# Attention steps of a fused attention and MLP kernel laid out from one table, with a pair's seven sums inverted together and transposes a turn later

## The chip, the cores and the metric

The kernel runs on one core of a Trainium2 chip. The metric is the device time of one execution in microseconds (us). A core has TensorE (PE; its weight loads are PEld), VectorE (DVE), ScalarE (ACT), GpSimd (POOL) and SyncE (SP), which issues most DMAs. Each engine works through its own instructions in the order in which the program holds them; between engines, semaphores keep the order.

## The reference

Causal attention over 2 batches of 12 heads, 448 positions and 64 values a head, followed by two MLPs on the 896 tokens of 768 values. All is float32.

```python
scores = scale * np.matmul(q, k.transpose(0, 1, 3, 2))      # scale = 1/8, masked above the diagonal
scores = scores - np.max(scores, axis=-1, keepdims=True)
attn = np.exp(scores)
attn = attn / (np.sum(attn, axis=-1, keepdims=True) + 1e-09)
x = np.matmul(attn, v)                                      # then laid out as 896 x 768
h = np.maximum(x @ w_in, 0.0);  x = h * h @ w_out           # first MLP, d_ff = 2048
h = x @ w_in2;  out = h * (1 / (1 + np.exp(-1.702 * h))) @ w_out2
```

## The kernel before

The attention works on 12 pairs of heads, `n = 12`. The rows of a pair's scores (448 queries by at most 448 keys) are cut into blocks of 128 queries, of which only the keys up to the diagonal are computed, and the blocks into three groups. Group 0 holds the third block (128 x 384) and the first (128 x 128) of each head, group 1 the second block (128 x 256) of each head, group 2 the last 64 queries of both heads at once (128 x 448). For pair 0 alone groups 3 and 4 hold the two blocks of group 0 apart. So a pair has seven tiles of scores; each has a column in the small tile `stat` for its maximum, its sum and the sum's reciprocal.

The stages of a pair, with the names of the code:

- `scores(p, g)`: TensorE multiplies q and k into PSUM banks named s (L231 for group 2, L238 for the others).
- `shifted(p, g)`: VectorE reads each tile out of PSUM, adds the mask, scales by -1/8, writes it to SBUF (`pnh`, for group 2 `pnl`) and keeps the row's minimum in `stat` (L266).
- `exponentials(p, g)`: ScalarE takes the exponential in place, with that minimum as the bias, and accumulates the row's sum in `stat` (L283).
- `normalise(p, gs)`: VectorE adds 1e-9 to the sums of the groups gs (L293) and inverts them (L294); GpSimd then multiplies each tile by its reciprocals (L296).
- `transpose(p, g)`, g = 0 and 1: TensorE transposes 32 pieces of the pair's probabilities into four PSUM banks named t (L311).
- `keep_transposed(p, g)`: two banks are copied to the tile `pt`, one by ScalarE and one by VectorE (L316).
- `values(p)`: TensorE multiplies `pt` with v into the bank x (L335). `keep_values` casts it on ScalarE (L347), and `keep_rest` keeps what the cast lost on VectorE (L351).

The program is written out pair by pair, and what is written is the order on each engine. Turn p of the loop holds scores, reductions and exponentials of pair p + 2, the rest of the normalisation of pair p + 1, the transposes and copies of pair p, and the product x of pair p - 1. Ahead of the loop stand all of pair 0 and pair 1 up to the exponentials.

PSUM has eight banks, handed out in the order in which they are asked for, so that an instruction that opens a bank waits until the reader of the bank's last owner is done. `pnh` and `pnl` have three buffers each: a reduction of pair p + 2 writes where the probabilities of pair p - 1 lay.

Two other kinds of work stand in the loop. `some(k)` issues k steps of the weight decode: int64 words of the MLP weights are turned into two float32 parts by VectorE (L106, L108, L100, L102) and ScalarE (L105, L101). Turns 3 to 8 hold two chunks' worth of steps, turns 10 and 11 two more. `filler(p)` issues, in turns 10 and 11 only, which have no scores left, products of the first MLP's first block (`first_term`: L125, L126, L127, three matmuls each). After the loop `first_product` and `second_product` of both MLPs follow, which are matmuls of these three lines with casts, activations and decode beside them.

Of the kernel before, what the change touches and what calls it, by code (L numbers as in the profile page):

```python
# [14 lines left out]
ALU = mybir.AluOpType  # L15
# [3 lines left out]
B, H, S, D = 2, 12, 448, 64  # L19
# [16 lines left out]
WARM = 7  # L36


@with_exitstack
def attention_mlps_kernel(  # L40
# [11 lines left out]
    nc = tc.nc  # L52
# [63 lines left out]
    X = {}  # L116
# [21 lines left out]
    with tc.tile_pool(name="const", bufs=1) as cp, tc.tile_pool(  # L138
# [119 lines left out]
        def shifted(p, g):  # L258
# [4 lines left out]
            work.sort(key=lambda u: u[0])  # L263
# [23 lines left out]
        def normalise(p, gs, eng=nc.gpsimd):  # L287
            if p >= n:
                return
            st = stat[p]  # L290
            work = [u for g in gs for k in range(1 if g == 2 else 2) for u in units(p, g, k)]
            lo, hi = min(u[3] for u in work), max(u[3] for u in work) + 1
            nc.vector.tensor_scalar(st[:, 2, lo:hi], st[:, 1, lo:hi], 1e-9, None, op0=ALU.add)  # L293
            nc.vector.reciprocal(st[:, 2, lo:hi], st[:, 2, lo:hi])  # L294
            for _, _, pn, s, _ in work:
                eng.tensor_scalar(pn, pn, st[:, 2, s : s + 1], 1.0, op0=ALU.mult, op1=ALU.mult)  # L296

        def transpose(p, g):

            if g == 0:  # L300
                PT[p] = qk_p.tile([128, 2, 1024], F32, tag="pt", name="pt")
# [12 lines left out]
        def keep_transposed(p, g):  # L314
            for k, tp in enumerate(tbank.pop((p, g))):
                (nc.vector.tensor_copy if k else nc.scalar.copy)(PT[p][:, k, 512 * g : 512 * g + 512], tp)  # L316
# [38 lines left out]
        for g in (3, 1, 4, 2):  # L355
            scores(0, g)
            shifted(0, g)
            exponentials(0, g)
            if g == 4:
                normalise(0, (3, 1))  # L360
        normalise(0, (4,))
        scores(1, 0)
        scores(1, 1)
        shifted(1, 0)
        normalise(0, (2,), nc.vector)
        exponentials(1, 0)
        scores(1, 2)
        shifted(1, 1)
        exponentials(1, 1)
        shifted(1, 2)  # L370
        exponentials(1, 2)
        normalise(1, (0,))
# [5 lines left out]
        def filler(p):  # L378
            if p + 2 >= n:
                first_term(0, *spare_terms.pop(0), X)  # L380

        def some(k):
            for _ in range(k):
                if decode:
                    decode.pop(0)()

        for p in range(n):
# [19 lines left out]
            some(many)  # L407
            filler(p)
            shifted(p + 2, 1)
            exponentials(p + 2, 1)  # L410
            keep_transposed(p, 1)
            normalise(p + 2, (0,))
            some(many - 1)
            if p > 0:
                values(p - 1)
                keep_values(p - 1)
            filler(p)
            scores(p + 2, 2)
            shifted(p + 2, 2)
            exponentials(p + 2, 2)  # L420
            if p > 0:
                keep_rest(p - 1)
            some(many)
            filler(p)
            some(many - 1)
        first_term(0, 5, 0, X)
        values(n - 1)
        while decode:
            decode.pop(0)()
        keep_values(n - 1)  # L430
        keep_rest(n - 1)
# [144 lines left out]
```

## Time and profile before

| | us |
|---|---|
| runs | 551.65, 551.95, 560.81 |
| median of the runs | 551.95 |
| profiled execution, its own time | 551.52 |
| its span | 549.7 |
| busy in the span: PE | 538.6 |
| DVE | 354.0 |
| ACT | 268.0 |
| POOL | 69.3 |

The profile is of one execution. Its span runs from the first to the last instruction; what lies around it is 1.8 us. A matmul's end is modelled, so matmuls that follow each other overlap in their rows, and a busy TensorE is not a TensorE at its peak: how long a step keeps TensorE is read from the start of one group to the start of the next. The attention takes the first sixth of the span, the MLPs the rest, in which TensorE has no gaps.

### The profile page before, as it was taken

To read this page: it belongs to the slowest core of one execution; us is meant where nothing else is said; L and a number is where in the kernel's file an instruction comes from. 1 tells how busy PE (TensorE), PEld (TensorE's weight loads), DVE (VectorE), ACT (ScalarE), POOL (GpSimd) and SP (SyncE) were. 2 spreads that over 40 slices of the span, in tenths; PEclk is the share of its full clock that TensorE was granted. 3 is DMA by queue.
4 is the path that set the end of the run, shared out by engine and by line. 5 is a ranking of instruction groups with operands and counts; after the bars stand their busy time and mean duration, and the time that the engine had idled before them with its cause. 6 is when DMAs were issued, how large, how long until landed. Compare 5 with 4: busy or idle time off the path is not lost.

```text
span 549.7 us, 8778 instructions
## 1 busy us (share of the span) xinstructions
PE 538.6 (98%) x3199; PEld 479.4 (87%) x3199; DVE 354.0 (64%) x806; ACT 268.0 (49%) x610; POOL 69.3 (13%) x115
## 2 busy tenths in 40 slices
PE   8998899999999999999999999999999999999997
PEld 4665678999999999999999999999999999999996
DVE  6988976666666667555465467888878874544420
ACT  6988855666666564233222264555555432222210
POOL 5765630000000000000000011222221100000000
PEclk9999999999999999999999999999999999999999
DMA  7862113343334434333332234334334363443000
GB/s 219 284 188 89 32 30 95 107 116 97 105 115 125 139 129 154 122 109 110 120 86 85 59 87 116 100 103 115 113 109 143 120 199 107 140 148 116 33 35 33
DMA packets 25018, 62.30 MB, mean 113 GB/s; under 512 B 4496, under 2 KB 9744, under 8 KB 24976
## 3 DMA queue, kind: packets, MB, share of 16 engines
q1 hardware_dynamic: 24256, 61.17, 36.6%
q10 hardware_dynamic: 720, 0.57, 0.3%
q8 instruction: 25, 0.41, 0.3%
q14 instruction: 17, 0.14, 0.1%
HBM read 58.98 MB, written 2.75 MB: 112 GB/s over the span
## 4 chain that ended last, share of the span: by engine, by line
PE 89%; ACT 6%; DVE 3%; issue 1%; DVEq 0%; ACTq 0%
PE h L125 14%; PE y L127 14%; PE y L126 14%; PE h L127 14%; PE h L126 14%; PE y L125 14%; ACT pnh L283 4%; DVE pnh L266 2%; PE x L335 1%; ACT pt L316 1%; PE s L238 1%; ACT x L347 1%; PE warm L220 1%; PE s L231 1%; PE t L311 0%
## 5 line engine op out<-in xcount | busy, mean ns | idle before, releaser
L101 ACT CAST wsplit<-m 128x384 fp32r<-128x384 f32 (+1 forms) x112 | 62.7, 560 | 241.5 <-PE y L127 128.4
L125 PE MATMUL h<-x,wsplit 128*128 128x448 f32 x384 | 141.1, 367 | 0.0
L125 PE MATMUL y<-h,wsplit 128*128 128x448 f32 x384 | 140.2, 365 | 0.0
L127 PE MATMUL y<-h,wsplit 128*128 128x448 f32 x384 | 140.2, 365 | 0.0
L126 PE MATMUL y<-h,wsplit 128*128 128x448 f32 x384 | 140.2, 365 | 0.0
L126 PE MATMUL h<-x,wsplit 128*128 128x448 f32 x384 | 140.2, 365 | 0.0
L127 PE MATMUL h<-x,wsplit 128*128 128x448 f32 x384 | 140.2, 365 | 0.0
L102 DVE TENSOR_TENSOR wsplit<-m,wsplit 128x384 fp32r<-128x384 f32 (+1 forms) x112 | 68.8, 614 | 64.1 <-ACT wsplit L101 64.0
L100 DVE CUSTOM_DVE_ANT_0 m<-m,e 128x768 uint16<-128x768 uint16 (+1 forms) x112 | 78.9, 704 | 47.4 <-ACT e L105 34.1
L125 PEld LDWEIGHTS h<-x,wsplit 128*128 128x128 f32 x384 | 72.1, 188 | 6.1 <-DVE stat L293 0.2
L126 PEld LDWEIGHTS h<-x,wsplit 128*128 128x128 f32 x384 | 72.1, 188 | 5.8 <-issue 0.2
L125 PEld LDWEIGHTS y<-h,wsplit 128*128 128x128 f32 x384 | 72.1, 188 | 5.7
L127 PEld LDWEIGHTS y<-h,wsplit 128*128 128x128 f32 x384 | 72.1, 188 | 5.7
L127 PEld LDWEIGHTS h<-x,wsplit 128*128 128x128 f32 x384 | 72.1, 188 | 5.7
L126 PEld LDWEIGHTS y<-h,wsplit 128*128 128x128 f32 x384 | 72.1, 188 | 5.7
L108 DVE SCALAR_TENSOR_TENSOR m<-wraw,m 128x384 uint32<-128x384 uint32 (+1 forms) x112 | 70.3, 628 | 0.0
L105 ACT ACTIVATE e<-wraw 128x384 uint32<-128x384 uint32 (+1 forms) x112 | 67.8, 605 | 0.0
L473 POOL TENSOR_TENSOR h<-g,h 128x448 fp32r<-128x448 f32 x16 | 24.0, 1499 | 336.8 <-ACT h L468 336.8
L106 DVE TENSOR_SCALAR m<-wraw 128x384 uint32<-128x384 uint32 (+1 forms) x112 | 42.6, 380 | 0.0
L283 ACT ACTIVATE pnh<-pnh,stat 128x128 f32<-128x128 f32 (+2 forms) x72 | 35.7, 497 | 7.4 <-DVE stat L266 7.2
L296 POOL TENSOR_SCALAR pnh<-pnh,stat 128x384 f32<-128x384 f32 (+2 forms) x72 | 34.6, 500 | 28.0 <-ACT pnh L283 18.7
L468 ACT CAST h<-g 128x448 fp32r<-128x448 f32 x64 | 34.1, 568 | 3.7 <-DVE g L466 3.5
(54 smaller groups left out, 372.4 us busy)
## 6 DMA issues: line engine op xcount, KB each, us to landing
wraw<-w1i SPq DMA_DIRECT2D x32, 384.0 KB, 3.1
wraw<-w1o SPq DMA_DIRECT2D x24, 512.0 KB, 3.7
wraw<-w2i SPq DMA_DIRECT2D x32, 384.0 KB, 3.1
wraw<-w2o SPq DMA_DIRECT2D x24, 512.0 KB, 3.8
kr<-kT SPq DMA_DIRECT2D x11, 224.0 KB, 3.9
yT<-o SPq DMA_DIRECT2D x11, 224.0 KB, 2.0
v<-v SPq DMA_DIRECT2D x6, 384.0 KB, 3.9
qr<-qT SPq DMA_DIRECT2D x10, 224.0 KB, 4.1
```

The costliest lines, as they stand in the source:

```text
L100: tt(out=m, in0=m, in1=e, op=ALU.add)
L101: nc.scalar.copy(s[:, 0, :], w)
L102: rests.append(lambda: tt(out=s[:, 1, :], in0=w, in1=s[:, 0, :].bitcast(F32), op=ALU.subtract))
L105: lambda: nc.scalar.mul(e, lo, 2.0**-29),
L106: lambda: ts(m, hi, 3, 0x3FFFFFFF, op0=ALU.logical_shift_left, op1=ALU.bitwise_and),
L108: lambda: stt(m, in0=hi, scalar=0xC0000000, in1=m, op0=ALU.bitwise_and, op1=ALU.bitwise_or),
L125: nc.tensor.matmul(ps, ws[:, 0, w], rhs[:, 0, b, :], start=first, stop=False)
L126: nc.tensor.matmul(ps, ws[:, 0, w], rhs[:, 1, b, :], start=False, stop=False)
L127: nc.tensor.matmul(ps, ws[:, 1, w], rhs[:, 0, b, :], start=False, stop=last)
L283: nc.scalar.activation(pn, pn, ACTF.Exp, bias=st[:, 0, s : s + 1], scale=-1.0, accum_out=st[:, 1, s : s + 1])
L296: eng.tensor_scalar(pn, pn, st[:, 2, s : s + 1], 1.0, op0=ALU.mult, op1=ALU.mult)
L468: nc.scalar.copy(h[:, 0, b, :], gs[b])
```

## The change

Instead of calls written out, two tables of steps hold the order, `PROLOGUE` for what stands ahead of the loop and `TURN` for one turn. A step is a name and a pair: in `PROLOGUE` the pair itself, in `TURN` its distance from the turn. The new function `do` issues a step once; `s`, `min`, `exp`, `add`, `rec`, `nrm`, `T`, `kT`, `x`, `xc` and `xr` are scores, reductions, exponentials, the addition of 1e-9, reciprocals, scalings, transposes, copies, the product and its two read-outs. A letter behind a name gives the engine: D is VectorE, A is ScalarE, M alternates between them by the pair's number; h orders the four reductions of group 0 by head.

What differs in a turn p:

- The exponentials of group 0 are those of pair p + 1, whose reductions stand in the turn before; so are the reduction and exponential of group 2 and the exponentials of group 1.
- The seven sums of a pair are added to once, on GpSimd, at the end of a turn (`add012`), and inverted once, on VectorE, in the next (`rec012`); the seven scalings then follow each other on GpSimd (`nrm012`). Pair 0 keeps its additions on VectorE and in three parts.
- Transposes and copies are of pair p - 1, the product and its read-outs of pair p - 2, each a turn later. Two turns without scores follow the loop, 12 and 13; turns 10 and 11 keep their first terms.
- Of a pair's four copies one alternates, so that VectorE has two for an even pair and three for an odd one.
- Pair 0 starts with group 1.

```diff
+PROLOGUE = (
+    ("s1", 0), ("s4", 0), ("s3", 0), ("min1", 0), ("min4", 0), ("exp1", 0), ("s1", 1), ("min3", 0), ("min1", 1),
...
+TURN = (
+    ("exp0", 1), ("some1", 0), ("fill", 0), ("min2", 1), ("rec012", 0), ("nrm012", 0), ("s0", 2), ("exp2", 1),
...
-        def shifted(p, g):
+        def shifted(p, g, by_head):
...
-            work.sort(key=lambda u: u[0])
+            if not by_head:
+                work.sort(key=lambda u: u[0])
...
-        def normalise(p, gs, eng=nc.gpsimd):
-            if p >= n:
-                return
-            st = stat[p]
+        def places(p, gs):
+
             work = [u for g in gs for k in range(1 if g == 2 else 2) for u in units(p, g, k)]
-            lo, hi = min(u[3] for u in work), max(u[3] for u in work) + 1
-            nc.vector.tensor_scalar(st[:, 2, lo:hi], st[:, 1, lo:hi], 1e-9, None, op0=ALU.add)
-            nc.vector.reciprocal(st[:, 2, lo:hi], st[:, 2, lo:hi])
-            for _, _, pn, s, _ in work:
-                eng.tensor_scalar(pn, pn, st[:, 2, s : s + 1], 1.0, op0=ALU.mult, op1=ALU.mult)
+            return work, slice(min(u[3] for u in work), max(u[3] for u in work) + 1)
+
+        def sums(p, gs, eng):
+            _, at = places(p, gs)
+            eng.tensor_scalar(stat[p][:, 2, at], stat[p][:, 1, at], 1e-9, None, op0=ALU.add)
+
+        def reciprocals(p, gs):
+            _, at = places(p, gs)
+            nc.vector.reciprocal(stat[p][:, 2, at], stat[p][:, 2, at])
+
+        def normalise(p, gs, eng):
+            for _, _, pn, s, _ in places(p, gs)[0]:
+                eng.tensor_scalar(pn, pn, stat[p][:, 2, s : s + 1], 1.0, op0=ALU.mult, op1=ALU.mult)
...
-        def keep_transposed(p, g):
-            for k, tp in enumerate(tbank.pop((p, g))):
-                (nc.vector.tensor_copy if k else nc.scalar.copy)(PT[p][:, k, 512 * g : 512 * g + 512], tp)
+        def keep_transposed(p, g, k, eng):
+            copy = nc.scalar.copy if eng == "A" or (eng == "M" and p % 2 == 0) else nc.vector.tensor_copy
+            copy(PT[p][:, k, 512 * g : 512 * g + 512], tbank[p, g][k])
...
-            many = 2 if p > 9 else 1
-            scores(p + 2, 0)
-            scores(p + 2, 1)
-            shifted(p + 2, 0)
-            normalise(p + 1, (1, 2))
-            exponentials(p + 2, 0)
-            filler(p)
-            transpose(p, 0)
-            transpose(p, 1)
-            keep_transposed(p, 0)
...
+            for step, lag in TURN:
+                if step == "fill":
+                    filler(p)
+                elif step.startswith("some"):
+                    some(int(step[4:]) * (1 if p < 10 else 3))
+                elif p:
+                    do(step, p + lag)
+                else:
+
+                    for q in range(lag + 1):
+                        if q or step.startswith(("T", "kT", "x")):
+                            do(step, q)
+        for p in (n, n + 1):
+            for step, lag in TURN:
+                if p + lag < n and not step.startswith(("some", "fill")):
+                    if p + lag == n - 1 and step == "x":
+                        while spare_terms:
+                            first_term(0, *spare_terms.pop(0), X)
+                        first_term(0, 5, 0, X)
+                    do(step, p + lag)
```

How the order moves shows in three places. VectorE, one turn before, from the reduction of group 2 to the next pair's (names with pnl are group 2, with pnh groups 0 and 1; stat holds the sums, stat_336 and stat_441 those of two pairs; the numbers behind names are the tiles'):

```order
L266 ISA pnl0_128,stat_336<-s_428,last_124 128x448
...
L351 TENSOR_TENSOR x_411<-x_412,x_411 128x448
L266 ISA pnh1_126,stat_441<-s_442,mask_123 128x384
...
L293 TENSOR_SCALAR stat_336<-stat_336 128x3
L294 RECIPROCAL stat_336<-stat_336 128x3
L316 COPY pt_465<-t_467 128x512
L266 ISA pnh1_126,stat_441<-s_448,mask_123 128x256
...
L316 COPY pt_465<-t_485 128x512
L293 TENSOR_SCALAR stat_441<-stat_441 128x4
L294 RECIPROCAL stat_441<-stat_441 128x4
L266 ISA pnl1_129,stat_441<-s_533,last_124 128x448
```

The same stretch now, in a turn with three copies, from one subtraction of x to the next:

```order
L374 TENSOR_TENSOR x_736<-x_737,x_736 128x448
L283 ISA pnl1_129,stat_685<-s_766,last_124 128x448
...
L315 RECIPROCAL stat_580<-stat_580 128x7
L339 COPY pt_802<-t_804 128x512
L283 ISA pnh2_127,stat_794<-s_795,mask_123 128x384
...
L339 COPY pt_802<-t_803 128x512
L339 COPY pt_802<-t_821 128x512
L122 TENSOR_SCALAR m_777<-wraw_354 128x384
L283 ISA pnh2_127,stat_794<-s_866,mask_123 128x256
...
L374 TENSOR_TENSOR x_845<-x_846,x_845 128x448
```

Between the subtraction of x (L351, now L374) and the first reduction of the next pair's group 0 there now stand a reduction of group 2, the one reciprocal, which is of another pair, and a copy; the two additions are gone. L122 is a step of the decode.

GpSimd, one pair's scalings now (before, the four of group 0 and the three others stood in two parts, and the addition was VectorE's):

```order
L311 TENSOR_SCALAR stat<-stat 128x7
L319 TENSOR_SCALAR pnh_125<-pnh_125,stat 128x384
L319 TENSOR_SCALAR pnh_125<-pnh_125,stat 128x128
...
L319 TENSOR_SCALAR pnh_125<-pnh_125,stat 128x256 x2
L319 TENSOR_SCALAR pnl_128<-pnl_128,stat 128x448
```

The addition for the next pair stands behind this pair's last scaling.

TensorE now, from the last score (L247) on, with t the transposes, x the attention's product and h the first MLP's first terms:

```order
L247 MATMUL s<-kr,ql_89 128x448
L141 MATMUL h_1185<-x,wsplit 128x448
...
L334 MATMUL t<-ident,pnh_125 128x64 x24
L334 MATMUL t<-ident,pnl_128 128x64 x8
L358 MATMUL x<-pt,v_95 64x384 x2
...
L334 MATMUL t<-ident,pnh_126 128x64 x24
L334 MATMUL t<-ident,pnl_129 128x64 x8
...
L334 MATMUL t<-ident,pnh_127 128x64 x24
L334 MATMUL t<-ident,pnl_130 128x64 x8
```

Three sets of transposes and four products, of which the first product stands here, now follow the last score, where two and three did.

## Rows read from the trace of the kernel before

**Rows 1.** Busy time by stretch (us; count of instructions), granted TensorE clock, DMA share, GB/s.

```profile
18.71:67.48 48.77, 44.30 (x593) 30.26 (x593) 43.50 (x176) 42.95 (x143) 28.62 (x57) 1.00 0.44 136
24.49:30.15 5.66, 5.43 (x74) 3.72 (x74) 5.00 (x22) 5.21 (x19) 3.39 (x7) 1.00 0.68 223
55.07:61.47 6.40, 5.44 (x75) 3.72 (x75) 6.13 (x24) 5.20 (x18) 3.99 (x7) 1.00 0.04 7
200.00:300.00 100.00, 100.00 (x495) 92.68 (x495) 57.81 (x102) 33.32 (x61) 0.00 (x0) 1.00 0.36 113
```

**Rows 2.** Timeline of TensorE: start us, duration us, line, idle before and what ended it.

```profile
4.28 2.04 PE L238 MATMUL s<-kr,qr 64*128 64x128 f32 x12
...
18.71 1.98 PE L335 MATMUL x<-pt,v 128*64 128x384 f32 x28 [0.45 <-DVE stat L266]
...
30.15 1.98 PE L335 MATMUL x<-pt,v 128*64 128x384 f32 x28 [0.23 <-DVE stat L266]
32.06 1.02 PE L231 MATMUL s<-kr,ql 128*128 128x448 f32 x2
33.01 1.57 PE L238 MATMUL s<-kr,qr 64*128 64x384 f32 x12
34.41 1.15 PE L311 MATMUL t<-ident,pnh 64*128 64x64 f32 x24
...
69.39 1.02 PE L231 MATMUL s<-kr,ql 128*128 128x448 f32 x2
...
84.61 0.47 PE L125 MATMUL h<-x,wsplit 128*128 128x448 f32 x1
```

**Rows 3.** Waits from 18.71 to 67.48: total us, times, longest.

```profile
ACT pnh L283 <- DVE stat L266: 5.8, 8, 1.2
PE x L335 <- DVE stat L266: 4.9, 9, 1.0
...
DVE x L351 <- ACT x L347: 2.5, 6, 0.5
```

**Rows 4.** Timeline of ScalarE and VectorE around the end of a turn.

```profile
46.35 0.53 ACT L347 CAST x<-x 128x448 fp32r<-128x448 f32 x1
...
46.91 0.62 DVE L351 TENSOR_TENSOR x<-x 128x448 fp32r<-128x448 f32 x1 [0.47 <-ACT x L347]
...
47.45 0.55 DVE L266 CUSTOM_DVE_ANT_0 pnh<-s,mask 128x384 f32<-128x384 f32 x1
...
48.04 0.61 ACT L283 ACTIVATE pnh<-pnh,stat 128x384 f32<-128x384 f32 x1 [0.50 <-DVE stat L266]
...
48.82 0.17 DVE L293 TENSOR_SCALAR stat<-stat 128x3 f32<-128x3 f32 x1
```

**Rows 5.** VectorE's groups, 18.71 to 67.48: count | busy us, mean ns | idle before.

```profile
L316 DVE COPY pt<-t 128x512 f32<-128x512 f32 x16 | 10.7, 672 | 0.0
L266 DVE CUSTOM_DVE_ANT_0 pnh<-s,mask 128x384 f32<-128x384 f32 x16 | 8.2, 550 | 0.0
L266 DVE CUSTOM_DVE_ANT_0 pnh<-s,mask 128x256 f32<-128x256 f32 x16 | 6.1, 414 | 0.0
L266 DVE CUSTOM_DVE_ANT_0 pnl<-s,last 128x448 f32<-128x448 f32 x8 | 5.0, 625 | 2.0 <-PE s L231 2.0
...
L266 DVE CUSTOM_DVE_ANT_0 pnh<-s,mask 128x128 f32<-128x128 f32 x17 | 4.3, 284 | 0.0
L108 DVE SCALAR_TENSOR_TENSOR m<-wraw,m 128x384 uint32<-128x384 uint32 x2 | 1.5, 738 | 0.0
L294 DVE RECIPROCAL stat<-stat 128x4 f32<-128x4 f32 x8 | 1.4, 178 | 0.3
...
L293 DVE TENSOR_SCALAR stat<-stat 128x4 f32<-128x4 f32 x8 | 1.4, 173 | 0.0
```

**Rows 6.** GpSimd's scalings (timeline), VectorE's reciprocal ahead of one, and GpSimd's small memset (groups).

```profile
43.35 1.23 POOL L296 TENSOR_SCALAR pnh<-pnh,stat 128x256 f32<-128x256 f32 x2 [2.24 <-ACT pnh L283]
...
49.37 0.94 POOL L296 TENSOR_SCALAR pnh<-pnh,stat 128x256 f32<-128x256 f32 x2 [1.51 <-ACT pnh L283]
50.27 0.65 POOL L296 TENSOR_SCALAR pnl<-pnl,stat 128x448 f32<-128x448 f32 x1
...
51.17 0.18 DVE L294 RECIPROCAL stat<-stat 128x4 f32<-128x4 f32 x1
...
51.54 1.84 POOL L296 TENSOR_SCALAR pnh<-pnh,stat 128x384 f32<-128x384 f32 x4 [0.63 <-ACT pnh L283]
...
L215 POOL MEMSET pnl<- 128x64 f32 x3 | 0.3, 152 | 0.0
```

**Rows 7.** Timeline of VectorE at the start.

```profile
5.22 0.29 DVE L266 CUSTOM_DVE_ANT_0 pnh<-s,mask 128x128 f32<-128x128 f32 x1 [3.54 <-PE s L238]
...
10.95 0.45 DVE L296 TENSOR_SCALAR pnl<-pnl,stat 128x448 f32<-128x448 f32 x1
```

More of the change, by code (lines that the diff above doesn't have):

```diff
@@ L36 @@
 WARM = 7
+PROLOGUE = (
[4 rows of a table added]
+)
+TURN = (
[4 rows of a table added]
+)
 @with_exitstack
@@ L285, in exponentials @@
                 )
-        def normalise(p, gs, eng=nc.gpsimd):
-            if p >= n:
-                return
-            st = stat[p]
+        def places(p, gs):
             work = [u for g in gs for k in range(1 if g == 2 else 2) for u in units(p, g, k)]
-            lo, hi = min(u[3] for u in work), max(u[3] for u in work) + 1
-            nc.vector.tensor_scalar(st[:, 2, lo:hi], st[:, 1, lo:hi], 1e-9, None, op0=ALU.add)
-            nc.vector.reciprocal(st[:, 2, lo:hi], st[:, 2, lo:hi])
-            for _, _, pn, s, _ in work:
-                eng.tensor_scalar(pn, pn, st[:, 2, s : s + 1], 1.0, op0=ALU.mult, op1=ALU.mult)
+            return work, slice(min(u[3] for u in work), max(u[3] for u in work) + 1)
[8 more added lines that the diff above has]
+                eng.tensor_scalar(pn, pn, stat[p][:, 2, s : s + 1], 1.0, op0=ALU.mult, op1=ALU.mult)
         def transpose(p, g):
-            if g == 0:
+            if p not in PT:
                 PT[p] = qk_p.tile([128, 2, 1024], F32, tag="pt", name="pt")
@@ L353, in keep_rest, with do @@
             )
[L355 to L372, printed above, removed]
+        done = set()
+        def do(step, p):
+            if not 0 <= p < n:
+                return
+            name = step.rstrip("ADMh")
+            kind, gs = name.rstrip("0123456789"), [int(g) for g in name if g.isdigit()]
+            if kind in ("add", "rec", "nrm"):
+                if any((kind, p, g) in done for g in gs):
+                    return
+                done.update((kind, p, g) for g in gs)
+            elif (name, p) in done:
+                return
+            done.add((name, p))
+            on_vector = step.endswith("D")
+            if kind == "s":
+                scores(p, gs[0])
+            elif kind == "min":
+                shifted(p, gs[0], step.endswith("h"))
+            elif kind == "exp":
+                exponentials(p, gs[0])
+            elif kind == "add":
+                sums(p, gs, nc.vector if on_vector else nc.gpsimd)
+            elif kind == "rec":
+                reciprocals(p, gs)
+            elif kind == "nrm":
+                normalise(p, gs, nc.vector if on_vector else nc.gpsimd)
+            elif kind == "T":
+                transpose(p, gs[0])
+            elif kind == "kT":
+                keep_transposed(p, *gs, step[-1])
+            else:
+                {"x": values, "xc": keep_values, "xr": keep_rest}[kind](p)
+        for step, p in PROLOGUE:
+            do(step, p)
         load_qk(3)
@@ L378, in filler @@
         def filler(p):
-            if p + 2 >= n:
+            if p + 2 >= n and spare_terms:
                 first_term(0, *spare_terms.pop(0), X)
@@ L396, in attention_mlps_kernel @@
                 decode += split_w_steps(len(wsplit)) + [lambda i=len(wsplit) + 3: load_w(i)]
-            many = 2 if p > 9 else 1
-            scores(p + 2, 0)
-            scores(p + 2, 1)
-            shifted(p + 2, 0)
-            normalise(p + 1, (1, 2))
-            exponentials(p + 2, 0)
-            filler(p)
-            transpose(p, 0)
-            transpose(p, 1)
-            keep_transposed(p, 0)
[L407 to L427, printed above, removed]
+            for step, lag in TURN:
[5 more added lines that the diff above has]
+                    do(step, p + lag)
+                else:
+                    for q in range(lag + 1):
[9 more added lines that the diff above has]
+                    do(step, p + lag)
         while decode:
             decode.pop(0)()
-        keep_values(n - 1)
-        keep_rest(n - 1)
     hp_ = ctx.enter_context(tc.tile_pool(name="hp_", bufs=KF))
```

6 rows, old and new, of tables (PROLOGUE, TURN) are left out of this document.

## The prediction

> **What bounds the kernel now.** I read first which engine is full in which stretch. From 200 to 300 us, inside the two MLPs, TensorE is busy for all 100 us at the full granted clock, 495 matmuls or 0.202 us each, and VectorE and ScalarE are far from full [rows 1]. The diff touches nothing there. From the end of the attention's last product, where the next matmul starts at 84.61 [rows 2], to the end of the span at 549.73 are 465.12 us, and I carry them over unchanged. What the change can win is idle time of TensorE before 84.61.
>
> I then looked at one turn of the pair loop, from one product x to the next. Eight turns take 48.77 us [rows 1], 6.10 each. In the stretch from 24.49 to 30.15 TensorE has 5.43 us of work, and I take this as the floor of a turn: the product 1.91 (30.15 to 32.06), the score of the last query block 0.95 (to 33.01), the other scores 1.40 (to 34.41) [rows 2], and the rest, 1.17, the transposes. So eight turns hold 48.77 - 8 x 5.43 = 5.3 us that TensorE could save.
>
> The waits say who holds it back: product x waits 4.9 us for VectorE (for a bank that the score reductions free), ScalarE's exponentials wait 5.8 us for VectorE, VectorE's x subtraction waits 2.5 us for ScalarE [rows 3]. In order of time it is one loop over two engines: the cast of x on ScalarE starts at 46.35, x's subtraction on VectorE waits for it until 46.91, the next pair's first reduction comes behind it at 47.45, and the exponential waits for that until 48.04, with ScalarE idle for 0.50 [rows 4]. ScalarE's busy 5.21 us a turn and VectorE's 5.00 [rows 1] are each under 5.43; it is the hand-over between them that makes 6.10.
>
> **The change part by part.** *The loop is cut.* Exponentials of group 0 now belong to the pair whose reductions ran a turn earlier, so they stand behind finished work, and the subtraction of x has a product two pairs old before it. Behind the subtraction on VectorE stand only the last reduction, the reciprocal and a copy.
>
> *VectorE's work.* A turn loses two additions (0.17 each) and one reciprocal (0.18) [rows 5]: 0.52. The copies go from two to three in every second turn: half of 0.67, +0.34 [rows 5]. Over the eight turns VectorE's 43.50 [rows 1] becomes about 42.0, or 5.25 a turn, under TensorE's floor. The weight decode makes turns uneven: the turn with two of its steps holds 6.13 of VectorE work against 5.00 without [rows 1]. A plain turn comes to 5.00 - 0.52 = 4.48 with two copies and 5.15 with three; a step of up to 0.74 [rows 5] on top makes 5.9, 0.5 over TensorE's 5.43. Three or four turns of the eight lie over it, and part of that is taken up by the slack of their neighbours.
>
> *ScalarE's work.* It loses half a copy a turn. It stands once a turn at the cast of x, whose product ends 0.93 + 1.17 + 1.91 = 4.0 us into TensorE's turn; the exponentials and the copy ahead of it are done by then, or some 0.1 late where a decode step is among them. This wait costs nothing while exp1, behind it, still reaches GpSimd before VectorE wants the reciprocal.
>
> *GpSimd.* Its seven scalings take 1.84 + 0.94 + 0.65 = 3.43, and its start comes 0.19 after the reciprocal's end (51.17 + 0.18 to 51.54) [rows 6]. The added addition on 128x7 is not in the trace; a 128x64 memset of 0.15 bounds it from below [rows 6], and half the pair of 128x256 scalings, 0.47 [rows 6], from above. I take 0.2, as it is nearest to the memset in size. The loop from reciprocal to reciprocal is then 0.18 + 0.19 + 3.43 + 0.2 + 0.19 = 4.2, or 4.5 with the upper price; both lie under 5.43, so it is covered. If ScalarE came late, VectorE would stand at the reciprocal with a copy, four reductions and a bank that TensorE needs behind it. The Trainium skill (GPSIMD Engine Reference, Engine selection) speaks against this move: elementwise work belongs on VectorE, GpSimd being about twice as slow with two inputs and about line rate with one. By that the addition would cost the row's 0.17 to 0.34, inside my bounds, and the sum would not change.
>
> *Transposes a turn later.* In the kernel before they wait for scalings that GpSimd gets late. Now the reciprocal stands about 1.2 us into a turn, so the scalings end near 4.8, and the transposes that need them come 5.43 + 0.93 = 6.4 us after its start. That gives 1.6 us of slack; the price if it goes is what is missing, on TensorE's path, in each turn.
>
> *The front.* VectorE's first reduction starts at 5.22 [rows 7], and I put it 0.4 later, since a 256-wide block now goes first. Its queue ahead of pair 1's reciprocal is three pairs of reductions, 23.6 us for eight pairs by the busy column or 2.95 each [rows 5], or 2.6 by group 0's four of 1.56, which ran in 1.37 start to start (47.45 to 48.82) [rows 4, 5]. To these come three additions, three reciprocals and one scaling of 0.45 [rows 7], 1.5 in all. That ends between 5.6 + 7.8 + 1.5 = 14.9 and 16.0; I take 14.9, as the reductions stand back to back as in that row. The reciprocal 0.18, a hand-over 0.19, scalings 3.43, the last eight of 32 transposes 0.3 and two more hand-overs 0.4 follow: x of pair 0 starts at 19.4 (19.0 to 20.3), against 18.71 before. But TensorE has by then also done a score of 0.95 and one of 0.93 (1.40 x 512/768) that came later before, so the front gains 18.71 + 1.88 - 19.4 = 1.2.
>
> *The tail.* After its last scores the kernel before needs 84.61 - (69.39 + 0.95) = 14.27 [rows 2] for two sets of transposes, three products and nine first terms. The changed order has one more set (1.17) and one more product (1.91) left: 17.35. They stand in front of the wait: the last pair's exponentials, reciprocal and scalings end about 10.7 us after the last score, and TensorE's work ahead of its transposes is 8 x 0.61 + 2 x 1.17 + 2 x 1.91 = 11.0. So I cost the longer drain at nothing, with only 0.3 us of cover; if it is gone, up to 3.4 us of scalings would show.
>
> *Sum.* A turn I put at 5.55: the floor of 5.43 and 0.12 for turns that VectorE fills over. There are now seven from the first product to that of the last turn with scores, then product and remaining scores 1.91 + 0.47 + 0.95. 19.4 + 7 x 5.55 + 3.33 + 17.35 + 465.12 = 544.05 of span. The profiled execution took 551.52 with a span of 549.73, so 1.8 lie around it, and its time is 0.4 under the median of the three runs, 551.95: **545.8 us**, about 1.1% less.
>
> **The rivals.**
> *The loop closes again (550 us).* VectorE and ScalarE are both within 0.3 us of the floor, and any hand-over that I have not seen eats it. For it: the decode turns that are 0.5 too full. Against: in the new order each wait has half a turn of slack. A turn of 6.10: 19.4 + 42.7 + 3.33 + 17.35 + 465.12 + 1.8 = 549.7, with the late front 550.6. Chance 19%.
>
> *GpSimd sets the turn (553.5 us, slower than before).* Place: the run of seven scalings, now between two reciprocals that VectorE waits for. The row for it: beside a decode step a pair of 128x256 scalings took 1.23 instead of 0.94 [rows 6], 0.29 more. GpSimd had idle time for this before; now the run is in a loop. Were all seven struck, it would be 3.43 + 7 x 0.29 = 5.46, and the loop 5.46 + 0.18 + 2 x 0.19 + 0.2 = 6.2, or 6.5 with the upper price. It decides from 5.43 on, so from four or five struck scalings a turn. With 6.3 a turn, 20.0 at the front and 1.8 that shows in the tail: 20.0 + 44.1 + 3.33 + 17.35 + 1.8 + 465.12 + 1.8 = 553.5. The Trainium skill (SBUF — State Buffer, two separate sides) gives the rule: VectorE, with two SBUF inputs or in a two-port mode, and GpSimd hold one port pair by turns, each for a whole instruction. The trace agrees in kind, 0.29 in a row. Reductions, copies and x read PSUM, so by it only decode steps strike. The rows say the same of how often: GpSimd's 28.62 in eight turns [rows 1] are 8 x 3.43 + 1.2, four strikes in all. Chance 8%.
>
> *TensorE without a gap (543 us).* Turns at 5.43, the front at 19.0 and a tail of 16.6, which is its pieces without switching: 19.0 + 38.0 + 3.33 + 16.6 + 465.12 + 1.8 = 543.9, and some 0.7 less if the front closes up too. Chance 9%.
>
> That the change does not do what its words say I leave out: the order shows one reciprocal over seven sums and transposes of the pair before.
>
> **How the numbers follow.** Forecast 62%, loop closes again 19%, no gap 9%, GpSimd 8%, something unseen 2%. The range takes in the forecast with its own bounds (543.5 to 547.5), most of the gapless case and the loop case to its late front: 543.0 to 550.6. Left out are about 5% below and 10% above. 2%, about what a measurement of this kernel can tell from no change, is 11.0 us. TensorE's own attention work is about 12 x 5.43 + 9 x 0.61 = 70.7, done between 4.28 and 84.61 [rows 2]: all its idle time is 9.6 us. So faster by over 2% has 3%; slower by over 2% (over 563) needs a turn of 7.4 us, 3%; within 2% the rest.
>
> **What would show it.** Right: products x 5.5 us apart from the second turn on; the waits of exponentials for VectorE and of x's subtraction for ScalarE gone or under 1 us in all; GpSimd in one run of seven a turn and its addition near 0.2; the first product near 19.4, the first MLP matmul behind the last product near 79. Wrong: VectorE standing at the reciprocal for GpSimd for more than 0.5 us a turn (then the first or second rival), transposes waiting for GpSimd, a gap of TensorE ahead of the last transposes, or the MLP part not 465 us long.

## The result: 547.0 us, and the profile after

Six runs of the changed kernel gave 546.32 to 547.61 us, median 546.96; six of the kernel before had the median 551.68. The ratio is 0.9916 (95% interval 0.9903 to 0.9929), a gain of 0.8%; the forecast was 545.8. The profiled execution took 547.05, with a span of 545.3. Some executions come out about 9 us longer, which two traces below show to lie in the matmuls of the MLPs (485 in 100 us for 496) and not in the attention, so ratios leave them out, and where they move a median the lowest run stands beside it.

Busy time by stretch in the changed kernel, against [rows 1]: seven turns, a turn with one step of the weight decode on VectorE, a turn with two, a piece of the MLPs. The columns are those of [rows 1].

```profile
20.57:59.49 38.92, 38.92 (x521) 25.76 (x519) 37.22 (x138) 35.11 (x120) 25.90 (x57) 1.00 0.52 157
26.13:31.69 5.56, 5.56 (x78) 3.68 (x75) 5.20 (x20) 5.06 (x17) 3.56 (x9) 1.00 0.91 278
42.81:48.37 5.56, 5.56 (x77) 3.68 (x75) 5.56 (x22) 5.56 (x21) 2.90 (x7) 1.00 0.15 49
200.00:300.00 100.00, 100.00 (x496) 92.68 (x495) 57.22 (x103) 30.95 (x56) 0.00 (x0) 1.00 0.37 113
```

TensorE is busy for all 38.92 us of the seven turns, where before it had 44.30 of 48.77. Each turn takes 5.56. Its timeline, against [rows 2]:

```profile
13.69 1.14 PE L254 MATMUL s<-kr,qr 64*128 64x384 f32 x8 [1.48 <-DVE stat L283]
...
18.50 1.14 PE L254 MATMUL s<-kr,qr 64*128 64x384 f32 x8 [1.23 <-DVE stat L283]
...
20.57 1.98 PE L358 MATMUL x<-pt,v 128*64 128x384 f32 x28
...
31.69 1.98 PE L358 MATMUL x<-pt,v 128*64 128x384 f32 x28
33.60 0.70 PE L254 MATMUL s<-kr,qr 64*128 64x256 f32 x4
34.23 1.02 PE L247 MATMUL s<-kr,ql 128*128 128x448 f32 x2
35.18 1.14 PE L254 MATMUL s<-kr,qr 64*128 64x384 f32 x8
36.15 0.92 PE L334 MATMUL t<-ident,pnh 64*128 64x64 f32 x24
...
37.25 1.98 PE L358 MATMUL x<-pt,v 128*64 128x384 f32 x28
...
62.03 1.02 PE L247 MATMUL s<-kr,ql 128*128 128x448 f32 x2
...
80.16 0.47 PE L141 MATMUL h<-x,wsplit 128*128 128x448 f32 x1
```

From start to start a turn is product 1.91, block 1's scores 0.63, the last group's 0.95, blocks 0's 0.97, transposes 1.10: 5.56 with no bracket, so no wait. The two score groups, 1.40 in one piece in [rows 2], cost 1.60 apart. The transposes last as long as before: 1.10 to the start of the next product, or 1.17 to their modelled end at 37.32, which is how the prediction's 1.17 was read. The two brackets left are in the front.

Waits from 20.57 to 62.98, against [rows 3]: those three are gone. GpSimd waits for the last exponentials and for the reciprocal, ScalarE for the products; in the whole list no engine waits for GpSimd, and no matmul for anything.

```profile
POOL stat L311 <- ACT pnh L300: 5.8, 7, 1.5
POOL pnh L319 <- DVE stat L315: 4.8, 5, 1.9
ACT x L370 <- PE x L358: 4.7, 6, 1.3
```

The sum of the prediction beside the trace: first product 20.57 for 19.4; seven turns 38.92 for 38.85; then to the end of the last scores (62.98) 3.49 for 3.33; tail 17.18 for 17.35; MLPs 465.1 for 465.12. The miss is the front's 1.17; the others cancel to within 0.1.

### The profile page after: what moved, and what is told of

Its sections match the earlier page's. It is cut to its first block, busy times and chain, and to the rows that moved or that the text cites. A ratio compares the mean times of both kernels' runs of the same rounds, so it can differ in the third digit from the quotient of the medians.

```text
span 545.3 us, 8723 instructions
## 1 busy us (share of the span) xinstructions
PE 538.0 (99%) x3199; PEld 478.0 (88%) x3199; DVE 352.6 (65%) x779; ACT 265.4 (49%) x604; POOL 73.1 (13%) x126
## 4 chain that ended last, share of the span: by engine, by line
PE 97%; DVE 2%; issue 0%; ACT 0%; ACTq 0%; DVEq 0%
PE h L141 14%; PE y L142 14%; PE h L143 14%; PE y L141 14%; PE h L142 14%; PE y L143 14%; PE x L358 4%; PE s L254 3%; PE t L334 2%; PE s L247 2%; DVE pnh L283 1%; PE warm L236 1%; DVE pnl L283 0%; DVE pt L339 0%; DVE stat L315 0%; DVE pnl L319 0%
## 5 line engine op out<-in xcount | busy, mean ns | idle before, releaser
L122 DVE TENSOR_SCALAR m<-wraw 128x384 uint32<-128x384 uint32 (+1 forms) x112 | 43.3, 387 | 0.0
L300 ACT ACTIVATE pnh<-pnh,stat 128x384 f32<-128x384 f32 (+2 forms) x72 | 35.6, 501 | 2.0 <-DVE stat L283 2.0
```

The lines of the kernel that those rows point to most:

```text
L122: lambda: ts(m, hi, 3, 0x3FFFFFFF, op0=ALU.logical_shift_left, op1=ALU.bitwise_and),
L300: nc.scalar.activation(pn, pn, ACTF.Exp, bias=st[:, 0, s : s + 1], scale=-1.0, accum_out=st[:, 1, s : s + 1])
```

## The experiments

Each is an edit of one of the two kernels. Two questions were open: which part took the turn from 6.10 to 5.56, and what held the front.

### The exponentials back in their own turn

```diff
-("exp0", 1), ("min2", 1), ... ("exp2", 1), ... ("exp1", 1), ... ("s2", 2)
+("min0h", 2), ("exp0", 2), ... ("min1", 2), ("exp1", 2), ... ("s2", 2), ("min2", 2), ("exp2", 2)
```

> The changed kernel with its exponentials back in the turn of their scores (each right behind the reduction of the same group, and the last group's reduction right behind its scores), everything else kept: sums on GpSimd in one go, transposes a turn later. Theory A (the prediction's): what held the turn of the kernel before at 6.10 us was the loop in which ScalarE's exponentials wait for VectorE's first reduction and VectorE's subtraction for ScalarE's copy of the products, and letting the exponentials lag by a turn is what cut it. Then ScalarE waits for VectorE again, some 5 us over the seven turns, and the turn is 5.75 to 6.1: 548.3 to 550.7. Rival B: the deeper pipeline of normalisation and transposes alone is what freed TensorE, the order of the exponentials is covered, the turn stays at 5.56 and the time at 547.0.

547.00 us, ratio 0.9913 (0.9898 to 0.9927). Seven turns took 38.92 again, and of the old waits this much came back (20.53 to 59.45):

```profile
DVE x L374 <- ACT x L370: 1.6, 3, 0.9
...
ACT pnh L300 <- DVE stat L283: 0.6, 1, 0.6
```

Rival B holds: the lag of the exponentials did not shorten the turn.

### The two score groups together

```diff
-("s0", 2), ("exp2", 1), ... ("exp1", 1), ("s1", 2),
+("s0", 2), ("s1", 2), ("exp2", 1), ... ("exp1", 1),
```

> The changed kernel with the scores of query block 1 put right behind those of blocks 0 (both groups of 64-row matmuls together, as in the kernel before), all else as it is. Theory A: the changed kernel's turn of 5.56 us is TensorE's own pace with no wait in it, and 0.20 of it comes from the two score groups standing apart (0.64 + 0.97 in the changed kernel against 1.40 together before). The turn falls to 5.36 to 5.43 us and the time by 7 x 0.13 to 0.20 us, to about 545.8. Rival B (the prediction's own reading): the 0.12 over 5.43 are turns that VectorE fills over, so the turn stays at 5.5 to 5.56 with TensorE now waiting for VectorE. Rival C: the earlier scores find their bank of PSUM not yet read, TensorE waits for VectorE's reductions, and the turn grows to 5.8 or more: 548.7 or more.

Ratio 0.9949 (0.9935 to 0.9964), about 548.8 us; the lowest run is 548.34. A turn of TensorE (of the next turn's products the last row holds the first two matmuls):

```profile
26.94 1.98 PE L358 MATMUL x<-pt,v 128*64 128x384 f32 x28 [0.28 <-DVE pt L339]
...
29.80 1.57 PE L254 MATMUL s<-kr,qr 64*128 64x384 f32 x12
31.21 0.91 PE L334 MATMUL t<-ident,pnh 64*128 64x64 f32 x24
...
32.65 0.54 PE L358 MATMUL x<-pt,v 128*64 128x384 f32 x2 [0.28 <-DVE pt L339]
```

The scores do take 1.41 in one piece, so Theory A's 0.20 is there, but the products stand 0.28 in five of the seven turns, and a turn is 5.71, 5.75 in the mean: TensorE waits for VectorE as in rivals B and C, at a size between theirs. What ends the wait is VectorE's copy of a transposed bank (26.20 to 26.89). The reductions that read the first scores run from 26.80 on and are not done when the products start at 26.94, so it was a bank of the transposes that was missing, not that of the first scores, as the expectation of the run with an earlier first reduction has it. All other parts of the change, without this one, bring about 2.8 of the 4.7 us.

### Block 1's scores behind the products, in the kernel before

```diff
             scores(p + 2, 0)
-            scores(p + 2, 1)
...
+            scores(p + 2, 1)      # and shifted, exponentials, normalise(p + 2, (0,))
             scores(p + 2, 2)
```

> The kernel before with one part of the change alone: the scores, reduction and exponentials of query block 1 come behind the products of the turn, not right behind the scores of block 0. Sums, reciprocals, scalings, the pair that a turn transposes and the place of the subtraction stay as before. Two runs have left this open: the exponentials back in their own turn cost nothing, and the two score groups together brought a TensorE wait of 0.29 us a turn at the first product back. Theory A: banks of PSUM are given out in turn, eight of them and ten requests a turn, so with both score groups ahead the products take the bank of the first scores of the same turn and must wait for their reduction on VectorE; with block 1 behind the products they take a bank that was read a turn ago. Then the wait of TensorE for VectorE ahead of the products (4.9 us over the turns) is gone, and the turn falls from 6.10 to 5.6 to 5.75 us: 548.2 to 549.2. Rival B (the prediction's loop): ScalarE's copy of the products, VectorE's subtraction, the first reduction and the first exponential still follow one another from turn to turn, and the turn stays at 6.0 to 6.1: 550.9 to 551.7.

547.04, ratio 0.9917 (0.9905 to 0.9929): the whole gain, from one part. Every turn from the first is 5.56, in the changed kernel's order and durations:

```profile
17.61 1.98 PE L335 MATMUL x<-pt,v 128*64 128x384 f32 x28
19.52 0.70 PE L238 MATMUL s<-kr,qr 64*128 64x256 f32 x4
20.16 1.02 PE L231 MATMUL s<-kr,ql 128*128 128x448 f32 x2
...
23.17 1.98 PE L335 MATMUL x<-pt,v 128*64 128x384 f32 x28
```

The edit moves three things: the order of TensorE's banks, the place of block 1's exponentials on ScalarE, and that of its reductions on VectorE, which come behind a copy. The next two runs take the first two one at a time.

### Banks alone: the first reductions head by head, in the kernel before

```diff
-            work.sort(key=lambda u: u[0])
+            if g or p < 2:
+                work.sort(key=lambda u: u[0])
```

> The kernel before with the four reductions of blocks 0 (and their exponentials) taken head by head from pair 2 on, so that the first head's bank, which the products take next, is read after two of the four (0.55 and 0.28 us) and not after three (two of 0.55 and one of 0.28); nothing else is moved. It shortens the way from the first reduction to the products by about 0.5 us and leaves the way through ScalarE as long as it was. Theory A, the loop that sets the turn of 6.10 us is closed by that bank (first reduction, products, copy on ScalarE, subtraction on VectorE, first reduction): the turn falls to about 5.65 and the time to about 548.4. Theory B, the loop is closed through ScalarE's own order (the first exponential waits for the first reduction, and the copy of the products stands behind that turn's exponentials): TensorE only waits less ahead of the products and more elsewhere, the turn stays at 6.0 to 6.1, 551 to 551.7.

Lowest run 551.25, ratio 0.9997 (0.9987 to 1.0008). Turns stay 6.10 (48.76 for eight). The subtraction on VectorE (L352; L348 is the cast, each a line later than before) and the transposes behind it:

```profile
46.83 0.62 DVE L352 TENSOR_TENSOR x<-x 128x448 fp32r<-128x448 f32 x1 [0.53 <-ACT x L348]
...
47.60 0.43 PE L312 MATMUL t<-ident,pnh 64*128 64x64 f32 x7 [0.44 <-DVE x L352]
```

The waits from 18.71 to 67.48:

```profile
DVE x L352 <- ACT x L348: 5.1, 8, 1.0
...
PE t L312 <- DVE x L352: 2.1, 6, 0.5
...
PE x L336 <- DVE stat L267: 1.5, 4, 0.6
```

Ahead of the products TensorE waits 1.5 us for VectorE instead of 4.9 [rows 3]. In its place stand 2.1 inside the transposes, for a bank that the subtraction still holds, and the subtraction waits 5.1 for ScalarE instead of 2.5. Theory B by the time. The chain that ended last, followed back from the last instruction through what released each step, does run over TensorE here in four of the eight turns, by the bank of the subtraction; so the run shows that the first scores' bank did not set the turn, not that no bank could.

### ScalarE's order alone: block 1's exponentials behind the copy of the products

```diff
-            exponentials(p + 2, 1)
             keep_transposed(p, 1)
...
                 keep_values(p - 1)
+            exponentials(p + 2, 1)
```

> The kernel before with one thing moved on ScalarE alone: the two exponentials of query block 1 come behind the copy of the products. The order of TensorE, of the banks and of VectorE stays. Theory A, the bank closes the loop: the products still wait for the first reduction, the turn stays at 6.0 to 6.1, 551 to 551.7. Theory B, ScalarE's order closes it: the copy of the products stood behind 0.99 us of those exponentials; it and the subtraction on VectorE come about 0.5 us earlier, since the subtraction stands behind the last group's reduction then; VectorE no longer waits for ScalarE there (2.5 us over the turns before), and the turn falls to 5.6 to 5.8: 548.2 to 549.6.

548.30, ratio 0.9942 (0.9930 to 0.9955): Theory B. From 18.96 to 58.80 seven turns take 5.69 each, 5.44 and 5.45 in the two without decode steps and 5.5 to 5.9 in the others. TensorE's products, the cast and the subtraction in a plain turn:

```profile
24.40 1.98 PE L335 MATMUL x<-pt,v 128*64 128x384 f32 x28
...
26.68 0.52 ACT L347 CAST x<-x 128x448 fp32r<-128x448 f32 x1
...
28.01 0.62 DVE L351 TENSOR_TENSOR x<-x 128x448 fp32r<-128x448 f32 x1
```

The cast starts 0.37 after the products' end (26.31), for 1.70 in the kernel before (cast at 46.35 [rows 4], products from 42.74 to the start of the next scores):

```profile
44.65 1.02 PE L231 MATMUL s<-kr,ql 128*128 128x448 f32 x2
```

The subtraction has no wait ahead of it. Busy time over the seven turns:

```profile
18.96:58.80 39.84, 38.00 (x518) 26.02 (x519) 37.31 (x154) 37.37 (x125) 25.46 (x50) 1.00 0.51 155
```

TensorE is busy for 38.00, 5.43 a turn. The other 0.26 a turn it stands, ahead of the products, for VectorE's reductions, in four of the turns with decode steps.

### That step undone in the changed kernel

```diff
-("x", -2), ("xc", -2), ("kT00M", -1), ("kT10D", -1), ("exp1", 1),
+("x", -2), ("kT00M", -1), ("kT10D", -1), ("exp1", 1), ("xc", -2),
```

> The changed kernel with ScalarE's copy of the products put back behind the two exponentials of query block 1, nothing else moved: the step that made the kernel before faster by itself, undone in the changed kernel. Theory A, that place is what cut the loop and the rest of the change does not: VectorE waits for ScalarE at the subtraction again and the turn grows to 5.7 to 6.1: 548 to 550.7. Theory B, the loop is cut twice in the changed kernel: its subtraction stands behind the reductions of block 1 and does not stand ahead of the first reduction, and the products take a bank that was read a turn earlier, so a later copy is covered: turn 5.56, 547.0.

546.95, ratio 0.9911 (0.9894 to 0.9927), every turn 5.56: Theory B. With block 1's scores behind the products, the later copy is covered.

### The extra turn taken out

```diff
-("rec012", 0), ("nrm012", 0), ... ("T0", -1), ... ("x", -2), ... ("add012", 1),
+("rec012", 1), ("nrm012", 1), ... ("T0", 0), ... ("x", -1), ... ("add012", 2),
```

> The changed kernel with its extra turn taken out: transposes in the pair's own turn and products one behind, as in the kernel before, exponentials in the turn of their scores; sums in one go, GpSimd's addition, the order of the score groups and of the copies kept. Theory A: the later transposes are what freed TensorE; without them a delay of ScalarE or VectorE reaches TensorE in the same turn again, and the turn is 5.7 to 6.1: 548 to 551. Rival B: the order within the turn is what counts and the extra turn nothing; the turn stays 5.56, the first product comes some 2 us earlier since it waits neither for a fourth pair's scores nor for its load, and one of the two gaps of the front (1.2 us) goes: about 545.8.

557.90, ratio 1.0112 (1.0097 to 1.0127), slower than the kernel before. Six turns from 26.87 take 6.47 each. Waits there:

```profile
POOL stat L311 <- ACT pnl L300: 14.2, 6, 2.9
DVE stat L315 <- POOL stat L311: 6.7, 6, 1.4
ACT pnh L300 <- POOL pnh L319: 6.4, 6, 1.3
```

One addition over seven sums can't start before the last exponential of its turn. VectorE then stands at the reciprocal for 1.1 us a turn with copies behind it, and ScalarE stands for GpSimd. So the later transposes pay for taking the sums in one go; with both, the changed kernel is no faster (546.96) than the kernel before with block 1's scores moved and neither (547.04).

### The addition on VectorE

```diff
-("add012", 1),
+("add012D", 1),
```

> The changed kernel with the addition to the seven sums put back on VectorE. Theory A: VectorE has room for it (5.25 us busy in a turn of 5.56, 0.15 us more makes 5.40), so the turn stays at 5.56 and the time at 547.0, and the move of this addition to GpSimd is worth nothing. Rival B: in VectorE's order the addition waits for the exponentials ahead of it and holds the reductions behind it, as the trace shows the addition on GpSimd waiting 0.8 us a turn for ScalarE; then VectorE stands up to 0.8 us a turn, TensorE waits for the bank of the next scores, and the turn grows to 5.7 to 6.3: 548 to 552.

547.70, lowest 547.31, ratio 0.9926 (0.9913 to 0.9938). Seven turns take 38.92 again: Theory A for the turn. The first product came 0.38 later in this run, in the front. The addition costs 0.161 us on VectorE and, first row, 0.284 on GpSimd (changed kernel, 20.57 to 59.49):

```profile
L311 POOL TENSOR_SCALAR stat<-stat 128x7 f32<-128x7 f32 x7 | 2.0, 284 | 5.8 <-ACT pnh L300 5.8
```

```profile
L311 DVE TENSOR_SCALAR stat<-stat 128x7 f32<-128x7 f32 x7 | 1.1, 161 | 0.0
```

The 0.284 is a mean: in six turns the addition takes 0.244 to 0.246, and once 0.517, from 52.56 on, beside a decode step of VectorE (52.43 to 52.97).

### More work on GpSimd

```diff
+            if len(gs) == 3:
+                for _ in range(2):
+                    eng.tensor_scalar(PNL[p % 3][:, :S], PNL[p % 3][:, :S], 1.0, 1.0, op0=ALU.mult, op1=ALU.mult)
```

> The changed kernel with two more scalings by 1.0 of the 128x448 tile on GpSimd each turn, 0.65 us each by the trace: GpSimd's work a turn goes from 3.8 to 5.1 us. Theory A: GpSimd's cover is at least 1.3 us (its last scaling ended at 45.47 in a turn whose transposes began at 47.27), so the turn stays at 5.56 and the time at 547.0. Rival B (the prediction's second rival): GpSimd's work stands in VectorE's way or makes the transposes wait, and the turn grows by 0.2 to 1.3 us: 548.4 to 556.

551.11, ratio 0.9994 (0.9985 to 1.0003): in between, with a span 3.6 us longer than the changed kernel's. Six of the seven turns are still 5.56 and one is 6.41. Another 2.0 us are lost in the tail, where TensorE has less to do:

```profile
78.72 0.46 PE L337 MATMUL t<-ident,pnl 64*128 64x64 f32 x8 [1.40 <-POOL pnl L322]
```

The last 0.7 lies in the front, where TensorE stands 2.20 us for the load of q of pair 3. It is not shown to be GpSimd's: the run with the later copy, which has no such work, stands 2.24 there, and its first product is as late (21.32 for 21.25).

### The score groups together, with a fourth buffer and an earlier first reduction

Against the run with the two score groups together (the lines that add the fourth buffer are not shown):

```diff
-("fill", 0), ("T0", -1), ("T1", -1), ("kT01D", -1), ("kT11A", -1), ("min0h", 2),
+("min0h", 2), ("fill", 0), ("T0", -1), ("T1", -1), ("kT01D", -1), ("kT11A", -1),
```

> The run with the two score groups together, with the reduction of blocks 0 moved ahead of the copies of the transposed blocks on VectorE (which takes a fourth buffer for the exponentials). Theory A: the 0.29 us that TensorE stood ahead of the products there was the bank of the first scores, read too late behind a copy; now it is read in time, TensorE's turn is its own work in this order, 1.91 + 0.95 + 1.40 + 1.17 = 5.43 us, and the time is 547.0 less 7 x 0.13, about 546.1. Rival B: VectorE (5.25 us a turn, more in turns with weight work) cannot keep up with 5.43, and the turn is 5.5 to 5.7: 546.6 to 548.

Lowest run 547.22; it is read by its trace, since one run decides nothing by its time. Four of the seven turns take 5.36 to 5.41, the three with two decode steps on VectorE 5.68 to 6.25. Busy time over the seven:

```profile
20.80:60.31 39.51, 38.50 (x518) 26.40 (x519) 38.03 (x140) 35.17 (x119) 25.98 (x57) 1.00 0.49 149
```

TensorE's own work is as short as Theory A said or shorter, and VectorE can't feed it evenly: rival B. Seven turns come to 39.51 for 38.92: putting the scores together saves TensorE's time and loses it again in waits.

### The loads of pairs 3 and 4 first

```diff
-        load_v(0, (0, 1))          # ahead of the prologue
...
         load_qk(3)
-        load_v(0, (2, 3))
+        load_v(0, (0, 1))
...
             load_qk(p + 4)
+            if p == 0:
+                load_v(0, (2, 3))
```

> The changed kernel with one thing moved: the loads of q and k of pairs 3 and 4 are queued ahead of the values of batch 0 (before, the values lay ahead of both). In the changed kernel TensorE stood for 1.48 us ahead of the scores of pair 3 (from 13.69) and for 1.23 us ahead of those of pair 4 (from 18.50). Theory A, those two gaps are the loads: q of pair 3 landed at 13.55 and q of pair 4 at 18.37, 0.13 us ahead of each restart. Then q of pair 3 lands near 10.6, the first gap closes, GpSimd's scalings of pair 0 (they ended at 15.07) become late next, the second gap closes, and the first product starts near 19.3 instead of 20.57: about 545.8 against the changed kernel's 547.0. Rival B, the reductions on VectorE that the trace names as what ended both gaps: they are not moved, the first product stays within 0.2 us of 20.57 and the time at 547.0. Turns stay 5.56 by both.

546.09, ratio 0.9897 (0.9883 to 0.9911): Theory A. In the changed kernel the two loads of q took 4.3 and 5.6 us from issue to landing:

```profile
9.28 0.43 SPq L171 DMA_DIRECT2D qr<-qT  x1
...
12.73 0.43 SPq L171 DMA_DIRECT2D qr<-qT  x1
```

```profile
qr<-qT SPq DMA_DIRECT2D x1, 224.0 KB, 4.3
...
qr<-qT SPq DMA_DIRECT2D x1, 224.0 KB, 5.6
```

With the loads first, the first of them (issued at 8.49):

```profile
qr<-qT SPq DMA_DIRECT2D x1, 224.0 KB, 2.7
```

9.28 + 4.3 = 13.6 and 12.73 + 5.6 = 18.3, just ahead of 13.69 and 18.50. TensorE in that run's front (lines are one lower):

```profile
12.16 1.14 PE L253 MATMUL s<-kr,qr 64*128 64x384 f32 x8
...
13.63 0.34 PE L333 MATMUL t<-ident,pnh 64*128 64x64 f32 x3 [0.28 <-DVE stat L282]
14.58 1.03 PE L333 MATMUL t<-ident,pnh 64*128 64x64 f32 x20 [0.61 <-POOL pnh L318]
...
17.22 1.14 PE L253 MATMUL s<-kr,qr 64*128 64x384 f32 x8
...
19.58 1.64 PE L357 MATMUL x<-pt,v 128*64 128x384 f32 x18
```

Both gaps are gone, pair 0's scalings are late next, and the first product is 0.99 earlier. Four runs above that keep the changed kernel's loads bear this out: at the first gap their traces name the load itself (1.06 to 2.24 us), and their first products come between 20.53 and 21.32.

### And pair 0's sums earlier

```diff
-("min2", 1), ("min0", 1), ("exp0", 1), ("add31D", 0), ("rec31", 0), ("nrm31", 0), ("add4D", 0), ("rec4", 0), ("nrm4", 0),
+("add314D", 0), ("rec314", 0), ("nrm314", 0), ("min2", 1), ("min0", 1), ("exp0", 1),
```

> The run with the loads of pairs 3 and 4 first, and beside it the sums and reciprocals of pair 0's first three score groups taken in one go and two reductions earlier on VectorE, so that GpSimd's scalings of pair 0 begin near 10.1 instead of 12.1. In the run with the loads alone TensorE stood 0.28 and 0.61 us inside the transposes of pair 0, for VectorE and for GpSimd. If GpSimd's late start is what is left of the front's gaps, the first product starts 0.6 to 0.9 earlier, near 18.8, and the time is about 545.2 to 545.4, faster than both kernels. If VectorE's work is (its reductions come later by what is put ahead of them), the first product stays near 19.6 and the time at 546.1.

545.97, lowest 545.36, ratio 0.9898 (0.9883 to 0.9912). The first product came at 18.85, but the next turn took 5.73. This run (545.36 to 546.06) and the one above (545.62 to 546.10) lie 0.2% below the changed kernel (546.32 to 547.61). The intervals of their ratios overlap with its own, so it is the earlier first product that shows the gain. The two can't be told apart. They are the fastest versions here.

## Why the prediction was right, step by step

**The bound and the loop: right.** The loop of four links over ScalarE and VectorE was what set 6.10. The chain that ended last in the kernel before holds no TensorE between 18 us and the products at 67.48; one turn of it (start and duration):

```profile
26.39 0.99 ACT pnh L283 x4
...
27.85 0.43 ACT x L347
...
28.31 0.23 DVE x L351
...
28.85 0.55 DVE pnh L266
...
29.44 0.92 ACT pnh L283 x3
```

ScalarE's work is on it from the first exponential to the cast, and the way over VectorE, from the cast's end at 28.28 to 29.44, comes on top. Moving the two exponentials of the first row behind the cast, on ScalarE alone, put their 0.99 us beside that way and brought 5.69; reading a bank sooner brought nothing. So TensorE's 4.9 us of waiting for banks was an effect of the loop, not its closing link.

**What cuts it: wrong.** The step said that exponentials of group 0 "stand behind finished work" and that the subtraction "has a product two pairs old before it". Taking the exponentials' lag away cost nothing, and the subtraction still follows its own product and cast within one turn, as before. What sufficed is the place of block 1's scores, reduction and exponentials behind the products, which the new `TURN` holds, which the list of what differs does not name, and to which the prediction gave no term. In the changed kernel the loop is cut more than once: without that place the rest still gave 2.8 of the 4.7 us, by which of its parts is not shown, and undoing the copy's place alone shows nothing either. That the subtraction no longer stands right ahead of the first reduction was not tried by itself. Nor is the last 0.13 separated (5.69 to 5.56): the edit that brings it moves the banks and both engines' order at once. The traces show only its parts, 5.43 of TensorE's work and 0.26 of waiting for the products' bank on one side, 5.56 of work and no wait on the other.

**The turn, 5.55: right size by luck, wrong cause.** The step was "the floor of 5.43 and 0.12 for turns that VectorE fills over". TensorE never waits in these turns; its own work here is 5.56. The floor was read 0.07 too long, by the modelled end of the transposes: start to start the old order takes 5.36, as the fastest turns of the run with a fourth buffer show. The two score groups apart add 0.20. A turn with one decode step on VectorE and a turn with two both take 5.56, though VectorE is busy for 5.20 in one and 5.56 in the other. The floor was that of an order that the change does not keep.

**GpSimd: right.** The addition is 0.245 in six turns of seven and 0.284 in the mean, inside 0.15 to 0.47, and no one waits for it. The Trainium skill (GPSIMD Engine Reference, Engine selection) puts such work on VectorE, though it gives GpSimd about line rate with one input; by the rows the addition costs 1.5 times as much there, 1.8 in the mean, so the measurement decides on the price. The time does not move, since neither engine sets the turn. Of GpSimd's work only two instructions in the seven turns were struck, that one addition and one scaling (0.90 for 0.48), where the second rival needed four or five a turn. The 1.3 us more were covered in six turns of seven, which bears out the 1.6 us of slack, but not in the tail: its cover was put at 0.3 us.

**Transposes a turn later: right that it costs nothing, wrong in its reason.** The step said that in the kernel before the transposes "wait for scalings that GpSimd gets late"; its trace has no wait of TensorE for GpSimd from 5 to 85 us. What needs the extra turn is the sums taken in one go.

**The front, 19.4: the mis-sized term.** It came to 20.57, past its upper bound of 20.3 (16.0 and the 4.5 that the step puts behind it make 20.5). The step counted VectorE's queue and GpSimd's scalings, and for TensorE two more scores; it did not ask when the q and k of those scores arrive. Pair 4's scores now stand ahead of the first product, and the loads set when they and pair 3's can start. With the loads first the product came at 19.58, so they are 0.99 of the 1.17, which is the difference of 545.8 to 547.0.

**Tail and MLPs: right**, within 0.2 us together. The sum names 0.4 us from the profiled execution to the median and does not add it; here that execution lay 0.1 over the median, so nothing hung on it.

## What to carry to other kernels

Where two engines hand work to each other round a loop, shorten the loop by moving the work that stands between two hand-overs on one engine; a wait seen on a third engine may be its shadow, as the chain that ended last showed. Before crediting each part of a change, put the cheapest part alone into the old kernel: here one part gave the whole gain, the others without it gave more than half, and two of them only paid for each other. When a deeper pipeline pulls work ahead, ask when its loads land.

## What the runs showed of the hardware

GpSimd's addition on 128x7 took 0.245 us for VectorE's 0.161, and 0.517 where VectorE ran a decode step beside it. The same twelve score matmuls of 64 rows cost TensorE 1.40 us in one piece and 1.60 in two. In a trace a wait can be put down to the wrong engine: both front gaps were named as VectorE's and went when only the order of the loads changed. Loads of 224 KB took 2.7 to 5.6 us to land in the front, with what was queued ahead of them.
